# A fused attention and feed-forward kernel: the first half of a weight product as plain float32 matmuls, and the order of the work searched again

## The chip, the cores and the metric

The kernel runs on one core of one Trainium2 chip. The metric is the device time of one execution in microseconds (us), from the runtime, and the median of several runs. A profile of one execution gives the span from the first to the last instruction and every instruction in it. Engines are named as in the profile: PE (matmul; PEld its weight loads), DVE, ACT, POOL, and SP, which here only issues DMAs.

## The reference, cut to what matters

```python
# q, k, v: (4, 8, 576, 64);  S = 576 tokens, D = 64, 4 x 576 = 2304 rows in all
q, k = rotate(q), rotate(k)                          # rotary embedding
attn = softmax(q @ k.T / 8)                          # per batch and head
x = heads_joined(attn @ v)                           # (2304, 512)
x = ((x @ w1) * (x @ w2)) @ w3 @ w_out               # w1, w2 (512, 1024), w3 (1024, 1024), w_out (1024, 512)
out = maximum(maximum(x @ v1, x @ v2), x @ v3) @ v_out   # (512, 768) x 3, then (768, 512)
```

All inputs are used at full precision: the weights reach the kernel as 64-bit words and the result is float32.

## The kernel before

**Products.** Every operand of a large matmul is split into two float32r tiles: HI, a rounded copy (ACT), and LO, what is left over (DVE or POOL, a subtraction). A product is then three matmuls, HI x HI, LO x HI and HI x LO (TERMS, line 42), summed in PSUM. Lines 372 and 373 issue all of them, so that the profile shows them as L373 and the tile names tell them apart. Transposes (L598) are matmuls of float32 tiles against the identity.

**Weights.** convert (line 418) loads a 128 x 512 chunk of 64-bit words into the tile raw (L376, 512 KB; two buffers), turns it to float32 in the tile cw by one ACT and two DVE instructions (L435, L437, L439), makes HI by an ACT copy (L441) and LO by a POOL subtraction (L443; later weights use DVE). Each raw buffer can be loaded again only when the DVE instruction L439 has read it.

**The fold.** Since nothing lies between w3 and w_out, the kernel multiplies these two first. The first half (fold, line 463) covers 512 of the 1024 inner columns: eight row blocks, each of four steps of three 128 x 512 matmuls, 96 in all, into the PSUM tile m. It reads four chunks of w_out (tiles wob in slots 4 and 5, named ws in the rows) and eight of w3 (w3b in slots 0 to 3). Its result goes to memory (wp_d) and the second half (fold_rest, line 764) adds to it much later. The same slots then take w1 and w2.

**Attention.** 16 pairs of heads are worked off one after the other. prepare (line 517) loads q and k and rotates them (tiles qk, and early for pair 1) into st; score (line 567) makes 128 x 576 scores in the tile s (two buffers of two PSUM banks each), of which DVE takes the maximum (L590, into sm) and ACT the exponential (L593, into p); move (line 620) transposes p into PSUM and splits it into pt (ACT L636, DVE L637); values (line 641) multiplies by v (L561 makes v's low part) into pv. inverse (line 600) turns the sums in sm into reciprocals (L603, L605) and transposes them. The first halves of the feed-forward layer (gates, line 486) run between the attention pieces, and the second layer follows after 480 us.

**The order.** Every instruction is a task with an engine, a modelled duration and a number prio. Plan.order (line 193) plays the tasks against the modelled engines and always takes the ready task with the smallest prio; the order in which tasks are taken is the order on each engine and in SP's queue, and every engine works strictly in that order. Plan.issue (line 281) first changes the prio numbers by a list of recorded random moves (MOVES, line 46; move, line 84), which an earlier search had found.

Of the kernel before, what the change touches and what calls it, by code (L numbers as in the profile page):

```python
# [10 lines left out]
F32 = mybir.dt.float32  # L11
F32R = mybir.dt.float32r
U32 = mybir.dt.uint32
AF = mybir.ActivationFunctionType
ALU = mybir.AluOpType
# [26 lines left out]
TERMS = ((HI, HI), (LO, HI), (HI, LO))  # L42
# [1 line left out]


MOVES = (
# [24 lines left out]
)  # L71


def draws(seed):
    mask = (1 << 64) - 1
    s = (seed * 0xD1342543DE82EF95 + 1) & mask
    while True:
        s = (s + 0x9E3779B97F4A7C15) & mask
        z = ((s ^ (s >> 30)) * 0xBF58476D1CE4E5B9) & mask
        z = ((z ^ (z >> 27)) * 0x94D049BB133111EB) & mask  # L80
        yield z ^ (z >> 31)


def move(prio, place, seed):

    d = draws(seed)

    def uni():
        return (next(d) >> 11) * (1.0 / 9007199254740992.0)

    by = (0.1, 0.3, 0.6, 1.5)[next(d) >> 62]
    share = (0.01, 0.03, 0.1, 0.3)[next(d) >> 62]
    parts = (1, 8, 32, 128)[next(d) >> 62]
    width = len(prio) / parts
    lo = uni() * (len(prio) + width) - width
    hi = lo + width
    if parts == 1:
        share *= 0.3
    for i in range(len(prio)):
        if lo <= place[i] < hi and uni() < share:  # L100
            x = uni() + uni() + uni() + uni() - 2.0
            prio[i] = prio[i] + by * 1.7 * x
# [33 lines left out]
class Plan:  # L136
# [6 lines left out]
    LAT = {"PE": 0.05, "ACT": 0.035, "DVE": 0.035, "POOL": 0.08, "SP": 0.1, "HOST": 0.0}  # L143
# [49 lines left out]
    def order(self, prio):  # L193

        tasks, LAT, LAP = self.tasks, self.LAT, self.LAP
        left = [len(k.deps) + len(k.after) for k in tasks]
        ready = [0.0] * len(tasks)
        users, last, slot = {}, {}, {}
        free, wait, live = {}, {}, {}
        for k in tasks:  # L200
            for b in k.shared:
# [2 lines left out]
                live[b.ring] = 0  # L204
                free.setdefault(b.ring.share, [(0.0, n) for n in range(b.ring.share.slots)])
                wait.setdefault(b.ring.share, [])
        clock = dict.fromkeys(LAT, 0.0)
        soon = {e: [] for e in clock}
        now = {e: [] for e in clock}
        dma, port, done = 0.0, 0.0, []  # L210
# [3 lines left out]
        while len(done) < len(tasks):  # L214
# [13 lines left out]
            while soon[e] and soon[e][0][0] <= at:  # L228
                n = heapq.heappop(soon[e])[1]
                heapq.heappush(now[e], (prio[n], n))  # L230
            k = tasks[heapq.heappop(now[e])[1]]
# [15 lines left out]
            end = at + k.dur  # L247
# [3 lines left out]
            if e == "PE":  # L251
                end += self.DRAIN
            if k.tail:
                dma = max(dma, end + 0.65) + 1.2 * k.tail
                end = dma + 0.8
            done.append(k)
            for b in k.shared:
# [10 lines left out]
            for o in k.out:  # L268
                t = clock[e] if e == o.eng == "PE" else end + LAT[o.eng]
# [39 lines left out]

def c_mm(n):  # L310
    return max(0.109, 0.013 + 0.000417 * n)


def c_act(n):
# [16 lines left out]
def fused_kernel(ctx, tc, qk, vv, cs, w3t, wo, w12, m2, wo2, out):  # L331
    nc = tc.nc
    pe, act, dve, pool, sync = nc.tensor, nc.scalar, nc.vector, nc.gpsimd, nc.sync
    plan = Plan()
    add = plan.add
# [12 lines left out]
    wpool = sb_pool(ctx, "wpool", side="right")  # L348
# [23 lines left out]
    def mm(o, a, b, start, stop, **kw):  # L372
        pe.matmul(o, a, b, start=start, stop=stop, **kw)  # L373
# [41 lines left out]
    def either(first):  # L415
        return ("DVE", c_dve, dve) if first else ("POOL", c_pool, pool)

    def convert(src, dst, c, prio, ring=None):

        raw, w = (ring or raw_r).new(), cw_r.new()  # L420

        def hi_word():
            return raw.t[:, :, 1]

        def low_word():
            return raw.t[:, :, 0]

        def u():
            return w.t.bitcast(U32)

        def cols():
            return dst.t[:, :, 512 * c:512 * c + 512]

        load(lambda: raw.t, lambda: src.rearrange("p (n t) -> p n t", t=2), 1.46, w=[raw], prio=prio)
        add("ACT", 0.68, lambda: act.activation(w.t, hi_word().bitcast(F32), **SHRINK),  # L435
            r=[raw], w=[w], prio=prio)
        add("DVE", 0.42, lambda: dve.tensor_scalar(low_word(), low_word(), 29, None, ALU.logical_shift_right),  # L437
            part=[raw], deps=raw.writers, prio=prio, lock=True)
        add("DVE", 0.69, lambda: dve.scalar_tensor_tensor(  # L439
            u(), u(), 3, low_word(), ALU.logical_shift_left, ALU.bitwise_or), r=[raw], w=[w], prio=prio, lock=True)  # L440
        add("ACT", c_act(512), lambda: act.copy(cols()[:, HI], w.t), r=[w], part=[dst], prio=prio)  # L441
        eng, cost, on = either(len(cw_r.all) > 28)
        add(eng, cost(512), lambda: on.tensor_tensor(cols()[:, LO], w.t, f32(cols()[:, HI]), ALU.subtract),  # L443
            r=[w, dst], part=[dst], prio=prio, lock=True)

# [8 lines left out]

    wob = [slots[4 + i].new() for i in range(2)]
    w3b = [slots[i].new() for i in range(4)]
    wp_done = []

    FILL = 1000.0
# [1 line left out]
    def fold(f):  # L463
        acc = m_r.new()
        for j in range(4):
            def go(j=j):
                w, o = w3b[f // 2].t, wob[j // 2].t
                for i, (s, t) in enumerate(TERMS):
                    mm(acc.t, w[:, s, 512 * (f % 2) + 128 * j:512 * (f % 2) + 128 * j + 128],
                       o[:, t, 512 * (j % 2):512 * (j % 2) + 512], j == 0 and i == 0, j == 3 and i == 2)  # L470
            add("PE", 3 * c_mm(512), go, r=[w3b[f // 2], wob[j // 2]], w=[acc], prio=6.0 + 2.6 * f)
        r = ga.new()
        add("ACT", c_evac(512), lambda: act.copy(r.t, acc.t), r=[acc], w=[r], prio=-1)
        wp_done.append(load(lambda: wp_d[f], lambda: r.t, 0.73, r=[r], prio=5))
# [241 lines left out]
            attend(p, part)  # L716
    attention = list(plan.tasks)

    for i in range(2):
        for c in range(2):  # L720
            convert(wo[:, 2 * i + c], wob[i], c, 3.0)
    for f in range(8):
        convert(w3t[f][:, 0], w3b[f // 2], f % 2, 17.0 + 2.2 * f)
        fold(f)
    for f in range(8):
        w12_convert(f)
# [390 lines left out]
```

## Time and profile before

| | us |
|---|---|
| three runs | 934.38, 935.26, 936.12 |
| median | 935.26 |
| the profiled execution, its own time | 933.76 |
| its span, first to last instruction | 931.7 |
| PE busy in the span | 892.7 (96%) |
| DVE, ACT, POOL busy | 601.5, 495.5, 397.6 |

The time of an execution is 2.1 us longer than its span. Matmuls are pipelined, so PE's busy time holds their latency where they overlap others, and the pitch from one matmul to the next has to be read from a run of equal matmuls. In the rows below, an entry in brackets is the idle time of an engine just before the row and what ended it.

### The profile page before, as it was taken

To read this page: it belongs to the slowest core of one execution; us is meant where nothing else is said; L and a number is where in the kernel's file an instruction comes from. 1 tells how busy PE (TensorE), PEld (TensorE's weight loads), DVE (VectorE), ACT (ScalarE), POOL (GpSimd) and SP (SyncE) were. 2 spreads that over 40 slices of the span, in tenths; PEclk is the share of its full clock that TensorE was granted. 3 is DMA by queue.
4 is the path that set the end of the run, shared out by engine and by line. 5 is a ranking of instruction groups with operands and counts; after the bars stand their busy time and mean duration, and the time that the engine had idled before them with its cause. 6 is when DMAs were issued, how large, how long until landed. Compare 5 with 4: busy or idle time off the path is not lost.

```text
span 931.7 us, 16391 instructions
## 1 busy us (share of the span) xinstructions
PE 892.7 (96%) x6018; PEld 836.9 (90%) x6018; DVE 601.5 (65%) x1048; ACT 495.5 (53%) x1108; POOL 397.6 (43%) x387
## 2 busy tenths in 40 slices
PE   2788989999999999999999999999999999999998
PEld 1577879998999999999998999999999999999886
DVE  6788888886666676567657233656788478578300
ACT  3688888886666667576655132534423333334411
POOL 2778887787745567352110000434653333232000
PEclk9799999999999999999999999999999999999999
DMA  7244556463322223311048343333333214155511
GB/s 276 85 126 164 177 187 200 128 188 101 100 91 75 69 84 99 100 41 32 27 146 273 117 142 92 103 101 96 91 91 130 63 46 147 46 184 175 214 62 68
DMA packets 61088, 110.32 MB, mean 118 GB/s; under 512 B 6736, under 2 KB 39760, under 8 KB 61008
## 3 DMA queue, kind: packets, MB, share of 16 engines
q1 hardware_dynamic: 61008, 109.28, 36.4%
q8 instruction: 47, 0.77, 0.4%
q14 instruction: 33, 0.27, 0.1%
HBM read 83.76 MB, written 25.50 MB: 117 GB/s over the span
## 4 chain that ended last, share of the span: by engine, by line
PE 86%; DVE 6%; ACT 2%; DMA 2%; issue 2%; POOL 1%; SPq 0%; DVEq 0%; ACTq 0%
PE q L373 46%; PE m L373 17%; PE t L598 9%; PE s L373 7%; PE pv L373 7%; DVE sm L590 1%; DVE pt L637 1%; ACT pt L636 1%; DVE cw L439 1%; DMA qk__118<-in_qk_dram 1%; DMA raw<-in_w_dram 1%; DVE raw L437 1%; DMA wq_d<-fl 1%; DVE early L542 0%; DMA wp<-wq_d 0%
## 5 line engine op out<-in xcount | busy, mean ns | idle before, releaser
L637 DVE TENSOR_TENSOR pt<-t,pt 128x320 fp32r<-128x320 f32 (+3 forms) x256 | 131.9, 527 | 58.4 <-ACT pt L636 54.1
L636 ACT CAST pt<-t 128x320 fp32r<-128x320 f32 (+3 forms) x256 | 112.5, 459 | 52.1 <-PE t L598 36.1
L373 PE MATMUL pv<-pt,v 128*128 128x256 f32 (+1 forms) x576 | 115.4, 317 | 4.5 <-DVE pt L637 3.6
L590 DVE TENSOR_REDUCE sm<-s 128x1 f32<-128x576 f32 x144 | 104.2, 749 | 17.3 <-PE s L373 16.4
L373 PE MATMUL q<-gt,wp 128*128 128x384 f32 x576 | 100.0, 334 | 0.0
L373 PEld LDWEIGHTS q<-gt,wp 128*128 128x128 f32 x576 | 99.8, 188 | 0.0
L373 PE MATMUL s<-st 64*128 64x288 f32 x768 | 74.2, 320 | 21.2 <-ACT st L548 13.1
L373 PEld LDWEIGHTS pv<-pt,v 128*128 128x128 f32 x576 | 83.5, 190 | 11.4 <-DVE pt L637 7.5
L373 PEld LDWEIGHTS s<-st 64*128 64x128 f32 x768 | 56.9, 193 | 35.3 <-ACT st L548 13.1
L959 ACT COPY tmp<-q 128x384 f32<-128x384 f32 x54 | 25.9, 480 | 92.6 <-PE q L373 92.1
L373 PE MATMUL q<-yc__7828,u 128*128 128x384 f32 x378 | 72.2, 340 | 0.0
L373 PE MATMUL q<-yc__8073,u 128*128 128x384 f32 x378 | 71.2, 340 | 0.0
L373 PE MATMUL q<-yc__7521,u 128*128 128x384 f32 x378 | 70.5, 340 | 0.0
L972 POOL TENSOR_TENSOR tmp<-tmp 128x384 f32<-128x384 f32 x27 | 30.2, 1119 | 86.9 <-ACT tmp L959 86.9
L373 PEld LDWEIGHTS q<-yc__8073,u 128*128 128x128 f32 x378 | 67.1, 188 | 0.1
L373 PEld LDWEIGHTS q<-yc__7828,u 128*128 128x128 f32 x378 | 67.2, 188 | 0.0
L373 PEld LDWEIGHTS q<-yc__7521,u 128*128 128x128 f32 x378 | 67.1, 188 | 0.0
L373 PE MATMUL q<-tail,tail 128*128 128x512 f32 x216 | 49.1, 389 | 0.0
L373 PEld LDWEIGHTS q<-tail,tail 128*128 128x128 f32 x216 | 40.5, 188 | 8.4
L985 DVE TENSOR_TENSOR tmp<-q,tmp 128x384 f32<-128x384 f32 x54 | 29.8, 554 | 16.3 <-PE q L373 16.2
L900 POOL TENSOR_TENSOR yx<-yc__7521 128x384 f32<-128x384 f32 x2 | 2.7, 1336 | 88.1 <-DVE yc__7521 L884 85.8
L1045 ACT COPY ga<-q 128x512 f32<-128x512 f32 x18 | 10.6, 588 | 54.8 <-PE q L373 46.7
(1282 smaller groups left out, 2149.9 us busy)
## 6 DMA issues: line engine op xcount, KB each, us to landing
gt<-g_d SPq DMA_DIRECT2D x24, 384.0 KB
raw<-in_m_dram SPq DMA_DIRECT2D x72, 128.0 KB
raw<-in_w_dram SPq DMA_DIRECT2D x16, 512.0 KB
h_d<-top SPq DMA_DIRECT2D x36, 192.0 KB
tail<-h_d SPq DMA_DIRECT2D x36, 192.0 KB
raw<-in_wo_dram SPq DMA_DIRECT2D x12, 512.0 KB
raw<-in_w3t_dram SPq DMA_DIRECT2D x12, 512.0 KB
vr<-in_vv_dram SPq DMA_DIRECT2D x16, 320.0 KB
```

What stands on the lines that cost most here:

```text
L373: pe.matmul(o, a, b, start=start, stop=stop, **kw)
L437: add("DVE", 0.42, lambda: dve.tensor_scalar(low_word(), low_word(), 29, None, ALU.logical_shift_right), part=[raw], deps=raw.writers, pri ...
L439: add("DVE", 0.69, lambda: dve.scalar_tensor_tensor(u(), u(), 3, low_word(), ALU.logical_shift_left, ALU.bitwise_or), r=[raw], w=[w], prio ...
L590: add("DVE", c_dve(S), lambda s=s, col=col: dve.tensor_reduce(sm.t[:, 0, col:col + 1], s.t[:, :, :288], axis=AX.XY, op=ALU.max, negate=Tru ...
L598: pe.transpose(o, x, ident.t)
L636: h = add("ACT", c_evac(n), lambda: act.copy(hi(), t.t[:rows, a:a + n]), r=[t], w=[pt], prio=prio)
L637: add("DVE", c_dve(n), lambda: dve.tensor_tensor(low(), t.t[:rows, a:a + n], f32(hi()), ALU.subtract), r=[t], part=[pt], deps=[h], prio=prio)
L900: k11 = add("POOL", c_pool(TN), lambda z=z, kk=kk: pool.tensor_tensor(z.t[:, 0], f32(yc.t[:, A11, kk, HI]), f32(yc.t[:, A11, kk, LO]), ALU ...
L959: add("ACT", c_evac(TN), lambda: act.copy(d.t, ps(o)), r=[accs[o]], w=[d], prio=prio)
L972: add("POOL", c_pool(TN), lambda: pool.tensor_tensor(s5.t, s1.t, s5.t, ALU.add), r=[s1], w=[s5], prio=prio)
L985: add("DVE", c_dve(TN), lambda: dve.tensor_tensor(e.t, ps(o), e.t, ALU.add), r=[accs[o]], w=[e], prio=prio)
L1045: add("ACT", c_evac(512), lambda acc=acc, o=o: act.copy(o.t, acc.t), r=[acc], w=[o], prio=P2 - 2)
```

## The change

The first half of the fold is computed by plain float32 matmuls: one instruction of 128 x 512 for each step in place of three, 32 in place of 96. convert gets an argument whole, with which the float32 word is written straight into the weight tile; the cw tile, the HI copy on ACT and the LO subtraction on POOL fall away for the twelve chunks of the fold. w_out's half now needs one slot (4) and w3's half two (0 and 1). The prio of w3's chunks goes from 17 + 2.2 f to 3 + 2.2 f, and the planner prices a fold step by a new function, c_whole. The planner's clocks start at 0.7, its DMA price per load changes, move knows a second kind of move (a shift of up to 128 consecutive tasks), and MOVES is a new list. The choice between DVE and POOL for later LO parts falls on the same chunks as before (28 and 16 count different tiles).

```diff
 MOVES = (
-    100000004, 100000005, 100000020, ...
+    30000018, 30000026, 30000042, ...
 )
...
 def move(prio, place, seed):
+    if next(d) >> 63:
+        by, width = (0.3, 1.0, 3.0, 10.0)[next(d) >> 62], 1 << (next(d) >> 61)
+        lo = int(uni() * (len(prio) + width)) - width
+        x = uni() + uni() + uni() + uni() - 2.0
+        for i in range(max(lo, 0), min(lo + width, len(prio))):
+            prio[i] = prio[i] + by * 1.7 * x
+        return
...
-        clock = dict.fromkeys(LAT, 0.0)
+        clock = dict.fromkeys(LAT, 0.7)
...
-                dma = max(dma, end + 0.65) + 1.2 * k.tail
+                dma = max(dma, end + 0.65)
+                dma += (1.9 if dma < 5.0 else 0.9) * k.tail
...
+def c_whole(n):
+    return 0.05 + 4 * 0.000417 * n
...
-    def convert(src, dst, c, prio, ring=None):
-        raw, w = (ring or raw_r).new(), cw_r.new()
+    def convert(src, dst, c, prio, ring=None, whole=False):
+        raw = (ring or raw_r).new()
+        w = None if whole else cw_r.new()
...
+        def word():
+            return dst.t[:, 512 * c:512 * c + 512] if whole else w.t
...
+        if whole:
+            return
         add("ACT", c_act(512), lambda: act.copy(cols()[:, HI], w.t), r=[w], part=[dst], prio=prio)
-        eng, cost, on = either(len(cw_r.all) > 28)
+        eng, cost, on = either(len(cw_r.all) > 16)
...
-    wob = [slots[4 + i].new() for i in range(2)]
-    w3b = [slots[i].new() for i in range(4)]
+    wob = slots[4].new(lambda slot: wpool.tile([128, 2048], F32, tag="ws4_0", name="wo"))
+    w3b = [slots[i].new(lambda slot, i=i: wlow.tile([128, 2048], F32, tag=f"ws{i}_0", name="w3")) for i in range(2)]
...
-                for i, (s, t) in enumerate(TERMS):
-                    mm(acc.t, w[:, s, 512 * (f % 2) + 128 * j:512 * (f % 2) + 128 * j + 128],
-                       o[:, t, 512 * (j % 2):512 * (j % 2) + 512], j == 0 and i == 0, j == 3 and i == 2)
-            add("PE", 3 * c_mm(512), go, r=[w3b[f // 2], wob[j // 2]], w=[acc], prio=6.0 + 2.6 * f)
+                c = 512 * (f % 4) + 128 * j
+                mm(acc.t, w3b[f // 4].t[:, c:c + 128], wob.t[:, 512 * j:512 * j + 512], j == 0, j == 3)
+            add("PE", c_whole(512), go, r=[w3b[f // 4], wob], w=[acc], prio=6.0 + 2.6 * f)
...
-        convert(w3t[f][:, 0], w3b[f // 2], f % 2, 17.0 + 2.2 * f)
+        convert(w3t[f][:, 0], w3b[f // 4], f % 4, 3.0 + 2.2 * f, whole=True)
```

How the instructions moved is shown at three places. Lines after the change are some 20 to 27 higher: L617 is the maximum (L590 before), L664 the low part of pt (L637), L588 that of v (L561), L464 and L466 the two DVE instructions of a weight word (L437, L439), L630 and L632 the reciprocal (L603, L605).

On DVE, in the last score of pair 0, there stood before:

```order
L590 TENSOR_REDUCE sm_175<-s_278 128x1
L637 TENSOR_TENSOR pt_308<-t_299,pt_308 64x256
L590 TENSOR_REDUCE sm_175<-s_279 128x1
L561 TENSOR_TENSOR v_211<-vr_153,v_211 128x10x64
L659 TENSOR_TENSOR x0__292<-pv_303,x0__292 64x256
L437 TENSOR_SCALAR raw_132<-raw_132 128x512
L590 TENSOR_REDUCE sm_175<-s_326 128x1
L439 SCALAR_TENSOR_TENSOR cw_202<-cw_202,raw_132 128x512
L437 TENSOR_SCALAR raw_179<-raw_179 128x512
L590 TENSOR_REDUCE sm_175<-s_327 128x1
```

Now the same two maxima (here of s_300 and s_301) stand there without them:

```order
L464 TENSOR_SCALAR raw_129<-raw_129 128x512
L664 TENSOR_TENSOR pt_285<-t_263,pt_285 128x512
L466 SCALAR_TENSOR_TENSOR wo_171<-wo_171,raw_129 128x512
L664 TENSOR_TENSOR pt_298<-t_289,pt_298 128x512
L617 TENSOR_REDUCE sm_175<-s_300 128x1
L664 TENSOR_TENSOR pt_326<-t_318,pt_326 64x256
L617 TENSOR_REDUCE sm_175<-s_301 128x1
```

Pair 1's v and the first weight word now come earlier on DVE, ahead of the first pt of pair 0:

```order
L464 TENSOR_SCALAR raw_127<-raw_127 128x512
L617 TENSOR_REDUCE sm_175<-s_209 128x1
L588 TENSOR_TENSOR v_224<-vr_201,v_224 128x10x64
L664 TENSOR_TENSOR pt_234<-t_219,pt_234 128x512
```

So the v and raw instructions that stood ahead of the maxima have moved out of the last score into the stretch before the first pt.

On PE, the first matmuls of the fold stood before behind the last transposes of pair 1's first half:

```order
L598 MATMUL t_648<-ident_111,p0__389 64x128
L598 MATMUL t_648<-ident_111,p1__473 64x128
L373 MATMUL pv_597<-pt_603,v_211 128x256
L373 MATMUL m_663<-ws4__177,ws0__558 128x512 x6
L373 MATMUL pv_677<-pt_618,v_211 128x256 x4
L373 MATMUL pv_677<-pt_654,v_211 128x256 x4
L373 MATMUL pv_677<-pt_657,v_211 128x256
```

Now the first two stand one head earlier:

```order
L625 MATMUL t_574<-ident_107,p0__399 128x128
L625 MATMUL t_574<-ident_107,p1__476 128x128
L393 MATMUL m_583<-wo_171,w3_508 128x512 x2
L393 MATMUL pv_596<-pt_539,v_224 128x256 x4
L393 MATMUL pv_596<-pt_563,v_224 128x256 x4
L393 MATMUL pv_596<-pt_581,v_224 128x256
```

The fold starts ahead of the head's values (pv_596) instead of behind those of the first head (pv_597).

On DVE, at the same place, the words of the fold stand so now (raw_547 and raw_566 reuse the buffers of raw_442 and raw_371, whose last readers are the two L466 here):

```order
L466 SCALAR_TENSOR_TENSOR w3_508<-w3_508,raw_442 128x512
L466 SCALAR_TENSOR_TENSOR wo_171<-wo_171,raw_371 128x512
L664 TENSOR_TENSOR pt_539<-t_531,pt_539 128x512
L664 TENSOR_TENSOR pt_563<-t_541,pt_563 128x512
L617 TENSOR_REDUCE sm_384<-s_549 128x1
L686 TENSOR_TENSOR x1__473<-pv_500,x1__473 64x256
L664 TENSOR_TENSOR pt_581<-t_570,pt_581 64x256
L686 TENSOR_TENSOR x1__473<-pv_500,x1__473 64x64
L617 TENSOR_REDUCE sm_384<-s_550 128x1
L464 TENSOR_SCALAR raw_547<-raw_547 128x512
L464 TENSOR_SCALAR raw_566<-raw_566 128x512
L664 TENSOR_TENSOR pt_617<-t_574,pt_617 128x512
```

Two L464 stand in a row with seven instructions between them and the second L466; before, two L437 (raw_560, raw_651) stood in a row a little later, just ahead of L603.

## Rows read from the trace of the kernel before

**Rows 1.** The page's first section: busy us, share of the span, instructions.

```profile
PE 892.7 (96%) x6018; PEld 836.9 (90%) x6018; DVE 601.5 (65%) x1048; ACT 495.5 (53%) x1108; POOL 397.6 (43%) x387
```

**Rows 2.** Busy us of each engine by stretch; the clock is PE's granted share.

```profile
core 0: us, PE busy (x) PEld busy (x) DVE busy (x) ACT busy (x) POOL busy (x), PEclk, DMA share, GB/s
...
13.14:34.00 20.86, 14.10 (x81) 11.11 (x81) 17.77 (x24) 12.85 (x28) 12.46 (x10) 1.00 0.32 128
34.00:38.00 4.00, 1.05 (x11) 0.82 (x11) 3.91 (x6) 1.48 (x4) 2.73 (x4) 0.78 0.29 82
38.00:50.00 12.00, 9.48 (x45) 7.72 (x46) 7.94 (x16) 7.66 (x19) 9.36 (x8) 0.50 0.67 215
50.00:72.20 22.20, 17.53 (x123) 13.64 (x123) 20.68 (x33) 17.46 (x42) 18.44 (x18) 1.00 0.40 124
72.20:124.00 51.80, 51.20 (x358) 43.16 (x360) 44.30 (x76) 45.40 (x111) 44.68 (x35) 1.00 0.50 162
124.00:150.00 26.00, 23.11 (x186) 20.00 (x184) 22.65 (x41) 22.35 (x56) 22.33 (x19) 1.00 0.51 166
150.00:480.00 330.00, 328.92 (x2710) 310.32 (x2708) 228.31 (x439) 229.67 (x576) 179.28 (x162) 1.00 0.30 93
480.00:519.00 39.00, 38.20 (x223) 34.47 (x224) 26.36 (x48) 17.69 (x30) 0.15 (x1) 1.00 0.80 263
519.00:928.00 409.00, 409.00 (x2292) 395.67 (x2292) 223.90 (x366) 135.66 (x240) 107.42 (x129) 1.00 0.34 108
```

**Rows 3.** Timeline of PE, 13 to 73 us: start, length, what, idle before.

```profile
13.14 0.61 PE L373 MATMUL s<-st 64*128 64x288 f32 x2 [13.14 <-ACT st L548]
...
23.12 1.78 PE L373 MATMUL s<-st,z__105 128*128 128x288 f32 x6 [3.38 <-ACT p__208 L593]
...
38.36 0.60 PE L373 MATMUL s<-st 64*128 64x288 f32 x1 [2.97 <-ACT p__349 L593]
...
64.37 1.64 PE L373 MATMUL m<-ws__177,ws__558 128*128 128x512 f32 x6 [0.28 <-DVE pt L637]
...
72.18 0.27 PE L598 MATMUL t<-ident,sm 128*9 128x128 f32 x1 [2.18 <-DVE sm L605]
```

**Rows 4.** Timeline of DVE, 26 to 70 us.

```profile
26.41 1.33 DVE L637 TENSOR_TENSOR pt<-t,pt 128x512 fp32r<-128x512 f32 x2 [2.30 <-ACT pt L636]
...
33.29 1.56 DVE L561 TENSOR_TENSOR v<-vr,v 128x640 fp32r<-128x640 f32 x1
...
35.35 1.30 DVE L437 TENSOR_SCALAR raw<-raw 128x512 uint32<-128x512 uint32 x1
36.68 0.76 DVE L590 TENSOR_REDUCE sm<-s 128x1 f32<-128x576 f32 x1
...
38.29 0.75 DVE L590 TENSOR_REDUCE sm<-s 128x1 f32<-128x576 f32 x1
...
67.06 2.92 DVE L437 TENSOR_SCALAR raw<-raw 128x512 uint32<-128x512 uint32 x2
```

**Rows 5.** Timeline of PE: two transposes, and the last run of 512-wide matmuls.

```profile
50.22 0.27 PE L598 MATMUL t<-ident,p__266 128*128 128x128 f32 x1
50.33 0.27 PE L598 MATMUL t<-ident,p__317 128*128 128x128 f32 x1
...
915.66 12.40 PE L373 MATMUL q<-tail 128*128 128x512 f32 x54
```

**Rows 6.** One fold tile's weight loads: instructions and form | busy, mean ns.

```profile
L373 PEld LDWEIGHTS m<-ws__177,ws__763 128*128 128x128 f32 x12 | 2.1, 188 | 0.4
```

**Rows 7.** Lines L443 (POOL) and L441 (ACT) alone, 0 to 119 us.

```profile
0.00:119.00 119.00, 0.00 (x0) 15.61 (x12) 0.94 0.50 165
...
0.00:119.00 119.00, 7.61 (x13) 0.94 0.50 165
```

**Rows 8.** A weight load in the chain that ended last, ACT's and PE's waits behind it.

```profile
125.39 5.86 DMA raw<-in_w_dram
...
131.34 0.66 ACT L435 ACTIVATE cw<-raw 128x512 f32<-128x512 f32 x1 [2.30 <-DMA raw<-in_w_dram]
...
132.87 0.42 PE L373 MATMUL pv<-pt,v 128*128 128x320 f32 x1 [1.36 <-DVE pt L637]
```

More of the change, by code (lines that the diff above doesn't have):

```diff
@@ L426, in low_word @@
             return raw.t[:, :, 0]
+        def word():
+            return dst.t[:, 512 * c:512 * c + 512] if whole else w.t
         def u():
-            return w.t.bitcast(U32)
+            return word().bitcast(U32)
+        own = dict(part=[dst]) if whole else dict(w=[w])
         def cols():
@@ L434, in convert @@
         load(lambda: raw.t, lambda: src.rearrange("p (n t) -> p n t", t=2), 1.46, w=[raw], prio=prio)
-        add("ACT", 0.68, lambda: act.activation(w.t, hi_word().bitcast(F32), **SHRINK),
-            r=[raw], w=[w], prio=prio)
+        add("ACT", 0.68, lambda: act.activation(word(), hi_word().bitcast(F32), **SHRINK),
+            r=[raw], prio=prio, **own)
+        first = plan.tasks[-1]
         add("DVE", 0.42, lambda: dve.tensor_scalar(low_word(), low_word(), 29, None, ALU.logical_shift_right),
@@ L439, in convert @@
         add("DVE", 0.69, lambda: dve.scalar_tensor_tensor(
-            u(), u(), 3, low_word(), ALU.logical_shift_left, ALU.bitwise_or), r=[raw], w=[w], prio=prio, lock=True)
+            u(), u(), 3, low_word(), ALU.logical_shift_left, ALU.bitwise_or), r=[raw], deps=[first], prio=prio, lock=True, **own)
+        if whole:
+            return
         add("ACT", c_act(512), lambda: act.copy(cols()[:, HI], w.t), r=[w], part=[dst], prio=prio)
-        eng, cost, on = either(len(cw_r.all) > 28)
+        eng, cost, on = either(len(cw_r.all) > 16)
         add(eng, cost(512), lambda: on.tensor_tensor(cols()[:, LO], w.t, f32(cols()[:, HI]), ALU.subtract),
@@ L466, in go @@
             def go(j=j):
-                w, o = w3b[f // 2].t, wob[j // 2].t
-                for i, (s, t) in enumerate(TERMS):
-                    mm(acc.t, w[:, s, 512 * (f % 2) + 128 * j:512 * (f % 2) + 128 * j + 128],
-                       o[:, t, 512 * (j % 2):512 * (j % 2) + 512], j == 0 and i == 0, j == 3 and i == 2)
-            add("PE", 3 * c_mm(512), go, r=[w3b[f // 2], wob[j // 2]], w=[acc], prio=6.0 + 2.6 * f)
+                c = 512 * (f % 4) + 128 * j
+                mm(acc.t, w3b[f // 4].t[:, c:c + 128], wob.t[:, 512 * j:512 * j + 512], j == 0, j == 3)
+            add("PE", c_whole(512), go, r=[w3b[f // 4], wob], w=[acc], prio=6.0 + 2.6 * f)
         r = ga.new()
@@ L717, in fused_kernel @@
     attention = list(plan.tasks)
-    for i in range(2):
-        for c in range(2):
-            convert(wo[:, 2 * i + c], wob[i], c, 3.0)
+    for c in range(4):
+        convert(wo[:, c], wob, c, 3.0, whole=True)
     for f in range(8):
-        convert(w3t[f][:, 0], w3b[f // 2], f % 2, 17.0 + 2.2 * f)
+        convert(w3t[f][:, 0], w3b[f // 4], f % 4, 3.0 + 2.2 * f, whole=True)
         fold(f)
```

55 rows, old and new, of the table MOVES are left out of this document.

## The prediction

> **What bounds the kernel now.** I read the busy table first. PE is busy for 96% of the span, every other engine for two thirds or less [rows 1]. Then the table by stretches: from 519 to 928 us PE has no idle time at all, from 150 to 480 us it has 330.00 - 328.92 = 1.1, from 480 to 519 us 0.8 [rows 2]. So from 150 us on PE sets the time, and whatever PE is late at 150 us it is late at the end. Ahead of 150 us it is not yet so. Nothing runs on PE before 13.14 us [rows 3]; from there it is idle for 20.86 - 14.10 = 6.8 us up to 34, 2.95 up to 38, 2.5 up to 50, 4.7 up to 72.2, 0.6 up to 124 and 2.9 up to 150, in all 20.4 us [rows 2]. Third, the clock in the same table: after the gap at 34 to 38 us the granted clock is 0.50, the lower level of 1.2 GHz, for the whole stretch from 38 to 50 us, in which PE is busy for 9.48 us; at the full level this work would take half, so the gap costs up to 4.7 us more. These 20.4 + 4.7 us are all that an order can win. Last, PE's and DVE's timelines, for who made PE wait: the maxima and exponentials of the scores (3.38 and 2.97 us), the reciprocal (2.18) [rows 3].
>
> **The change part by part.**
>
> *The matmuls.* A run of 54 matmuls of the fold's shape takes 12.40 us; without one latency of 0.39 at its end (53 pitches) that is 12.01 / 53 = 0.227 us each [rows 5]. The 96 that go cost 96 x 0.227 = 21.8 us of PE. What one plain float32 matmul of that shape costs no row shows. The nearest rows on the cheap side are the float32 transposes, which start 0.11 us apart (50.22, 50.33) for 128 columns [rows 5]: for 512 columns 0.44 us, 32 x 0.44 = 14.1, a gain of 7.7. On the dear side, a product of two numbers that each have two parts has four partial products, of which the old form computed three; at the pitch of a pass 4 x 0.227 = 0.91 us, 32 x 0.91 = 29.1, a loss of 7.3. Dearer still, if each of the four had to load its weights in the open at 0.188 us [rows 6]: 4 x 0.415 = 1.66 us, 53.1, a loss of 31.3. I take 0.91: the fold's own row has the same shape and the same operands, while a transpose multiplies by ones and zeros. The Trainium skill (FP8 and Floating Point Precision, Matmul Precision) says that true FP32 takes four passes through the array, which speaks against this change; by it the matmuls cost +7.3, by the transposes' row -7.7, and no row of the kernel before decides it.
>
> *What the conversion saves.* Twelve LO subtractions on POOL go, 15.6 us, and twelve HI copies on ACT, 12 x 7.61 / 13 = 7.0 us [rows 7]. Neither engine is the bound: in the stretch 72.2 to 124 us PE itself has 0.6 us idle [rows 2]. I count them only where a wait passes through them, below. DVE's two instructions per word stay, and SP's loads are as many as before.
>
> *The gap at 34 to 38 us.* Before, DVE makes v (1.56 us) and shifts a weight word (1.30) right ahead of the maximum at 36.68, and more weight work ahead of the second at 38.29 [rows 4]; PE waits 2.97 us for the exponential behind the first [rows 3]. Now these instructions stand ahead of the first pt, where DVE was idle for 2.30 us [rows 4]. That cover is nearly enough: v and one shift need 2.86. The maxima follow the scores directly. Of 2.95 us idle I take 2 away (bounds 1 to 2.95), since a maximum (0.75) and an exponential still lie between two scores. The clock then need not fall: 3 of 4.7 us (0 to 4.7). If the gap returns elsewhere, both terms are gone.
>
> *The start, 13 to 34 us.* PE's first score waits for the same loads and rotations, so the 13.14 us stay. Two rotations of pair 1 have moved ahead of the first maximum, where they delay it by about one instruction, and one fewer stands ahead of the second. I take 1 us of the 6.8 (-1 to 3).
>
> *38 to 50 us.* The waits there are behind maxima and pt at half clock: 1 of 2.5 (0 to 2).
>
> *50 to 72.2 us.* The first fold matmuls run at 64.37 us [rows 3]: words, then the ACT copy, then POOL. Without the last two they can follow DVE directly, and they stand one head earlier, with one more right ahead of the transposed reciprocal, which waited 2.18 us [rows 3] behind two weight shifts of 2.92 us [rows 4]. Filler of 0.91 us a piece covers most of it: 2.5 of 4.7 (1 to 4).
>
> *72.2 to 150 us.* The waits at 126 to 138 us hang on a weight load that lands 5.86 us after its issue and holds ACT for 2.30, PE then for 1.36 [rows 8]. With POOL and ACT lighter and PE with more to do, 1.5 of 3.5 (0 to 3).
>
> *After 150 us* the set of instructions is the same and PE is full: 0.
>
> *The sum.* Won: 2 + 3 + 1 + 1 + 2.5 + 1.5 = 11.0 us (bounds 1 to 19.7). Lost: 7.3. Net -3.7. The profiled execution took 933.76 us, so it would take 930.1; the median of the runs is 1.5 higher, so 935.26 - 3.7 = 931.6 us.
>
> **The rivals.**
>
> *Loads in the way (slower).* Now two weight shifts stand in a row on DVE behind seven instructions, and their loads can only be issued when the two L466 ahead of these have read the buffers. Two pt of 0.67, two maxima of 0.75 and three short ones are some 4.1 us; a load took 5.86 us to land [rows 8]. DVE would then stand for some 2 us, with pt and the next maxima behind it, hence PE. The eight words of w3 go through the two buffers in four such turns: 4 x 2.2 = 8.8, so 931.6 + 8.8 = 940.4. It decides as soon as a load takes longer than DVE's work between. For it: the old kernel shows just this on ACT [rows 8]. Against: POOL and ACT no longer hold a word back, and PE has its filler ready by then.
>
> *Half the gain.* The waits of the first 70 us are replaced by others and only some 7 of the 11 us come: 7.3 is lost, 935 us, no change. For it: DVE does the same work up to the first fold matmul as before, and it is busy 20.68 of 22.2 us from 50 to 72 [rows 2].
>
> *The float32 matmul is cheap.* At the transposes' price the change doesn't pay on PE at all: 935.26 - 11.0 - 7.7 = 916.6.
>
> *The float32 matmul is dear*, with its weight loads in the open: 935.26 - 11.0 + 31.3 = 955.6.
>
> *All the waits go*: 935.26 + 7.3 - 19.7 = 922.9.
>
> **How the numbers follow.** A measurement of this kernel can tell about 0.2%, 1.9 us, from no change. Chances: the forecast, 926.5 to 933.4 us, 0.50; all waits gone, below 926.5, 0.05; cheap matmul 0.04; half the gain, within 1.9 us of 935.26, 0.17; loads in the way or as much lost by another wait, 937.1 to 942, 0.20; dear matmul 0.04. Faster 0.59, same 0.17, slower 0.24. The range 925 to 940.5 leaves out the cheap and the dear matmul and the outer edges of their neighbours, under 0.2.
>
> **What would show it.** In the profile after: fold matmuls with a pitch of 0.91 us (0.44 and 1.66 are the others); no fall of the clock between 38 and 50 us and no PE wait of 2.97 us ahead of pair 0's last exponentials; the first fold matmul before 60 us; PE idle between 13 and 150 us near 12 us instead of 20.4; and 150 to 928 us as long as before. I am wrong if DVE waits for raw loads between 50 and 100 us, if a clock of 0.50 shows up at another place, or if PE is no longer full after 150 us.

## The result and the profile after

| | us, median | ratio to before, 95% interval |
|---|---|---|
| before | 934.8 | |
| after | 944.1 | 1.0104 [1.0077, 1.0132] |
| after, measured again beside other kernels | 948.1 | 1.0154 [1.0112, 1.0195] |
| predicted | 931.6 (925 to 940.5) | 0.996 |

The kernel after is slower by 9 us, where 4 us of gain were forecast. The profiled execution took 945.02 us (before 933.76), 11.3 more. Its table by stretches, with the bounds of [rows 2] (columns: bounds, length, then for each engine busy time and count, at the end the granted clock, the DMA share and GB/s):

```profile
13.14:34.00 20.86, 14.77 (x84) 12.02 (x83) 19.30 (x24) 11.22 (x26) 14.68 (x12) 1.00 0.30 109
34.00:38.00 4.00, 2.77 (x22) 2.15 (x20) 3.56 (x6) 3.90 (x9) 3.30 (x3) 0.95 0.66 176
38.00:50.00 12.00, 10.02 (x69) 8.62 (x68) 11.36 (x22) 8.53 (x23) 9.29 (x9) 0.87 0.59 198
50.00:72.20 22.20, 18.98 (x123) 12.87 (x121) 17.72 (x30) 15.58 (x38) 15.57 (x14) 1.00 0.56 183
72.20:124.00 51.80, 47.91 (x285) 32.43 (x284) 42.17 (x75) 39.27 (x95) 30.25 (x26) 1.00 0.48 158
124.00:150.00 26.00, 23.69 (x174) 18.69 (x173) 19.08 (x34) 19.94 (x50) 17.55 (x18) 1.00 0.36 124
150.00:480.00 330.00, 326.62 (x2677) 306.27 (x2676) 229.93 (x436) 229.41 (x577) 177.62 (x161) 1.00 0.29 92
480.00:519.00 39.00, 37.05 (x245) 34.48 (x244) 19.55 (x39) 14.92 (x30) 1.76 (x2) 1.00 0.55 179
519.00:928.00 409.00, 407.27 (x2275) 392.56 (x2274) 234.12 (x380) 138.06 (x246) 106.78 (x129) 1.00 0.36 115
```

Read the difference of length and PE's busy time, row by row, against [rows 2]. Up to 72.2 us PE is idle less than before, as forecast. The mean granted clock from 38 to 50 us is 0.87 where it was 0.50; it still falls to the lower level of 1.2 GHz, but for the first 3 us of this stretch only:

```profile
38.00:41.00 3.00, 2.50 (x14) 2.15 (x13) 2.88 (x7) 1.03 (x4) 1.62 (x3) 0.50 0.95 315
41.00:50.00 9.00, 7.52 (x57) 6.47 (x57) 8.48 (x15) 7.50 (x21) 7.66 (x7) 1.00 0.47 160
```

From 72.2 to 124 us it is idle for 3.9 us (before 0.6), from 150 to 480 for 3.4 (1.1), from 480 to 519 for 1.95 (0.8), from 519 to 928 for 1.7 (none).

The turning point shows when PE's matmuls are counted off in the timelines: the start of the same work, in us. A pair of heads has 54 score matmuls, so the scores of pair 2 (pairs are counted from 0) start with the 109th. The last two columns are kernels of the experiments, both with after's computation: in the order of before, and in an order made with loads priced at 4.8 us.

| start of | before | after | order of before | priced at 4.8 us |
|---|---|---|---|---|
| the fold | 64.4 | 53.8 | 62.8 | 54.0 |
| scores of pair 2 | 67.7 | 62.4 | 66.6 | 64.7 |
| scores of pair 4 | 123.7 | 126.0 | 128.8 | 119.3 |
| the products of x | 480.4 | 487.1 | 486.2 | 475.4 |
| the products of gt, the gated result | 554.2 | 563.9 | 560.9 | 548.5 |
| the products with v1 to v3 | 654.1 | 664.4 | 660.7 | 648.4 |
| the last product | 853.4 | 863.8 | 860.0 | 847.7 |

After is 5.3 us ahead of before at the scores of pair 2, 2.3 behind at those of pair 4, 6.7 at the products of x and 9.7 at those of gt. The loss is made between 62 and 564 us.

PE's timeline after has the gap of [rows 3] closed: the two waits in front of the scores at 36 us are 0.47 and 0.40 us.

```profile
36.24 0.40 PE L393 MATMUL s<-st 64*128 64x288 f32 x1 [0.47 <-ACT p__332 L620]
37.04 1.35 PE L393 MATMUL s<-st 64*128 64x288 f32 x11 [0.40 <-ACT p__332 L620]
...
65.45 1.88 PE L393 MATMUL m<-wo,w 128*128 128x512 f32 x4
...
71.03 0.33 PE L625 MATMUL t<-ident,p__589 128*128 128x128 f32 x1 [1.75 <-DVE pt L664]
...
71.71 1.02 PE L393 MATMUL m<-wo,w 128*128 128x512 f32 x2
...
109.69 0.33 PE L625 MATMUL t<-ident,p__864 128*128 128x128 f32 x1 [1.98 <-DVE pt L664]
```

The row at 65.45 is the fold. Each float32 matmul stands in the trace as two records (PE has 5986 records, 32 fewer than before, for 32 matmuls in place of 96); four records take 1.88 us, so the pitch of one is (1.88 - 0.59) / 3 = 0.43 us (0.59 is the time of a single one) and a matmul costs 0.86 us. All 32 cost 27.5 us, against 21.8 for the 96 [rows 5].

The waits at 71.03 and 109.69 are new, both for pt from DVE. What held DVE is in its own timeline:

```profile
56.44 0.43 DVE L464 TENSOR_SCALAR raw<-raw 128x512 uint32<-128x512 uint32 x1
57.08 0.43 DVE L464 TENSOR_SCALAR raw<-raw 128x512 uint32<-128x512 uint32 x1 [0.22 <-DMA raw<-in_w3t_dram]
...
61.59 1.76 DVE L466 SCALAR_TENSOR_TENSOR w<-w,raw 128x512 uint32<-128x512 uint32 x1
...
66.24 0.49 DVE L664 TENSOR_TENSOR pt<-t,pt 128x320 fp32r<-128x320 f32 x1
69.91 0.67 DVE L464 TENSOR_SCALAR raw<-raw 128x512 uint32<-128x512 uint32 x1 [3.18 <-DMA raw<-in_w3t_dram]
70.50 0.48 DVE L664 TENSOR_TENSOR pt<-t,pt 128x320 fp32r<-128x320 f32 x1
...
93.38 0.69 DVE L466 SCALAR_TENSOR_TENSOR w<-w,raw 128x512 uint32<-128x512 uint32 x1
...
108.22 1.02 DVE L464 TENSOR_SCALAR raw<-raw 128x512 uint32<-128x512 uint32 x1 [3.32 <-DMA raw<-in_w_dram]
...
126.17 0.43 DVE L464 TENSOR_SCALAR raw<-raw 128x512 uint32<-128x512 uint32 x1 [2.97 <-DMA raw<-in_w_dram]
```

At 61.59 DVE reads the last of a raw buffer; SP issues the next load into it at once, at 63.39, and it lands 6.50 us later. DVE has 3.4 us of other work, then stands for 3.18 us at the word's first instruction, and pt, for which PE waits, is queued behind it. The waits at 108.22 and 126.17 are of the same kind, but for words of w1 and w2 (in_w_dram); the last word of the fold was read at 93.38.

Two lists of the trace of after follow. First the chain of waits: some of the transfers among its longest pieces, from 60 to 130 us and from 150 to 560 us (start, duration, what).

```profile
63.39 6.50 DMA raw<-in_w3t_dram
72.42 4.00 DMA raw<-in_w3t_dram
102.25 5.88 DMA raw<-in_w_dram
121.44 4.63 DMA raw<-in_w_dram
...
153.78 6.64 DMA g_d<-ga
303.30 5.35 DMA qk__3968<-in_qk_dram
...
490.30 6.71 DMA raw<-in_w3t_dram
499.14 6.11 DMA rawc<-in_w3t_dram
507.74 3.74 DMA rawc<-in_w3t_dram
514.00 4.15 DMA g_d<-ga
```

Then the tile raw from 55 to 135 us: how long DVE and ACT sat idle until a weight load had landed (us, times), 14.4 us in all, more than half of it for the words of w1 and w2.

```profile
  DMA raw<-in_w_dram: 8.0, 5
  DMA raw<-in_w3t_dram: 6.4, 6
```

The transfers lie on the path that sets the end, and not the weight words alone: results on their way to memory (g_d), q and k (qk), and the second half of the weights (rawc) at 490 to 512 us. A 512 KB load takes 3.74 to 6.71 us there. The order was made by a planner that takes such a load to land 0.42 + 0.65 + 0.9 x 1.46 + 0.8 = 3.2 us after SP takes it up; the planner of before, with 1.2 in place of 0.9, took 3.6. So the diff has three changes in one: the float32 fold, a new order, and a lower price for all but the first transfers, under which that order was made. The Trainium skill (DMA: Bandwidth & Descriptors, Anatomy of one DMA) gives 2.0 us and the bytes over 436 GB/s for a transfer issued by GpSimd, by estimate also 3.2 us for 512 KB; these loads are issued by SP, and the trace has 3.74 to 6.71 us, so here it would be too little.

### The profile page after: what moved, and what is told of

Its sections match the earlier page's. It is cut to its first block, busy times and chain, and to the rows that moved or that the text cites. A ratio compares the mean times of both kernels' runs of the same rounds, so it can differ in the third digit from the quotient of the medians.

```text
span 943.2 us, 16297 instructions
## 1 busy us (share of the span) xinstructions
PE 901.0 (96%) x5986; PEld 829.6 (88%) x5986; DVE 602.8 (64%) x1048; ACT 487.2 (52%) x1096; POOL 377.6 (40%) x375
## 4 chain that ended last, share of the span: by engine, by line
PE 75%; DMA 10%; DVE 6%; ACT 3%; issue 3%; POOL 2%; SPq 1%; ACTq 0%; DVEq 0%; POOLq 0%
PE q L393 41%; PE m L393 14%; PE t L625 7%; PE pv L393 6%; PE s L393 6%; DMA raw<-in_w3t_dram 2%; DMA g_d<-ga 1%; DMA raw<-in_wo_dram 1%; DVE pt L664 1%; ACT pt L663 1%; DMA raw<-in_w_dram 1%; DMA rawc<-in_w3t_dram 1%; DMA rb<-r_d 1%; SPq L396 1%; DVE cw L466 1%
## 5 line engine op out<-in xcount | busy, mean ns | idle before, releaser
L664 DVE TENSOR_TENSOR pt<-t,pt 128x320 fp32r<-128x320 f32 (+3 forms) x256 | 132.3, 527 | 63.3 <-ACT pt L663 60.0
L617 DVE TENSOR_REDUCE sm<-s 128x1 f32<-128x576 f32 x144 | 104.1, 751 | 19.2 <-PE s L393 18.1
L479 DVE TENSOR_TENSOR gt<-gt 128x768 fp32r<-128x768 f32 x24 | 25.5, 1062 | 36.8 <-ACT gt L478 36.8
L478 ACT CAST gt<-gt 128x768 fp32r<-128x768 f32 x24 | 20.1, 836 | 43.8 <-DMA gt<-g_d 36.8
```

Of the source, the lines that this page charges most:

```text
L478: add("ACT", c_act(n), lambda: act.copy(sel()[:, HI], f32(sel()[:, LO])), r=[dst], part=[dst], prio=prio)
L479: add(eng, c_dve(n) if eng == "DVE" else c_pool(n), lambda: e.tensor_tensor(sel()[:, LO], f32(sel()[:, LO]), f32(sel()[:, HI]), ALU.subtract),
L617: add("DVE", c_dve(S), lambda s=s, col=col: dve.tensor_reduce(sm.t[:, 0, col:col + 1], s.t[:, :, :288], axis=AX.XY, op=ALU.max, negate=Tru ...
L664: add("DVE", c_dve(n), lambda: dve.tensor_tensor(low(), t.t[:rows, a:a + n], f32(hi()), ALU.subtract), r=[t], part=[pt], deps=[h], prio=prio)
```

## Experiments: the matmuls and the order apart

In each, "before" ran on the same chip; ratios are to it.

**The order of before with float32 matmuls.**

```diff
-                for i, (s, t) in enumerate(TERMS):
-                    mm(acc.t, w[:, s, 512 * (f % 2) + 128 * j:512 * (f % 2) + 128 * j + 128],
-                       o[:, t, 512 * (j % 2):512 * (j % 2) + 512], j == 0 and i == 0, j == 3 and i == 2)
+                mm(acc.t, f32(w[:, HI, 512 * (f % 2) + 128 * j:512 * (f % 2) + 128 * j + 128]),
+                   f32(o[:, HI, 512 * (j % 2):512 * (j % 2) + 512]), j == 0, j == 3)
```

> The order of the kernel before, kept instruction for instruction; only the three matmuls of each fold step (96 in all) become one plain float32 matmul (32) on the same tiles, read as float32. The copies to HI and the subtractions to LO stay; what they hold beyond HI is left out of the product, so a part of the computation is changed. Theory 1, the price of the float32 matmuls goes to the end in any order: the trace of after has 0.86 us for each, 32 x 0.86 = 27.5 against 21.8 before, so 934.8 + 5.7 = 940.5. Theory 2, the weight loads are what costs (the new order's wait for them): here the loads are where they were, and PE's longer work hides some of the old waits between 64 and 150 us (about 5 us of idle there), so 936 to 938. Theory 3, the new order is itself the worse one: as theory 1, at most 940.5.

Measured 939.2 us, 1.0066 [1.0045, 1.0088], which is 4 to 8 us more: the 5.7 us read from the trace of after lie in it. In the old order the matmuls' price goes to the end.

**The order of before with the whole change in computation.**

```diff
-        add("ACT", c_act(512), lambda: act.copy(cols()[:, HI], w.t), r=[w], part=[dst], prio=prio)
+        add("ACT", c_act(512), (lambda: None) if whole else lambda: act.copy(cols()[:, HI], w.t), r=[w], part=[dst], prio=prio)
...
-            convert(wo[:, 2 * i + c], wob[i], c, 3.0)
+            convert(wo[:, 2 * i + c], wob[i], c, 3.0, whole=True)
```

> The whole change in what is computed (32 float32 matmuls, no HI copies and no LO subtractions for the twelve words of the fold), in the order of the kernel before. Against the run with the HI and LO work kept, it prices the relief of ScalarE (7.0 us) and GpSimd (15.6 us). If that relief is worth nothing, as PE sets the time, 940.5 or the same as that run; if the waits on words between 50 and 150 us go by it, 936. The kernel after measured 944.1: whatever this run takes less than that is what the order searched anew costs. Theory 1 (price alone): 939 to 941, order 3 to 5. Theory 2 (loads in the way): the same, but with no wait of PE behind a weight load between 60 and 130 us. Theory 3 (order worse by itself, anywhere): the same time, with the order's loss after 130 us.

Measured 938.0 us, 1.0053 [1.0033, 1.0073]. That is 1 us below what was expected of theory 1; "before" took 933.1 us on this chip, 1.7 less than the expectation started from. The relief of ACT and POOL is worth about 1 us as long as the order stays, within the intervals nothing. After is at 1.0104 and 1.0154, so the new order costs some 5 to 9 us although its first 70 us are better. The table of starts has the same: against this run after leads by 4.2 us at the scores of pair 2 and by 2.8 at those of pair 4, and is behind by 0.9 at the products of x, by 3.0 at those of gt and by 3.8 at the last. Here neither DVE nor ACT waits for a weight word between 55 and 135 us, and PE is idle for 2.7 us from 150 to 928 us, in after for 7.1.

**The new order with three cheap matmuls.** Here the fold's product is another one: the words' upper halves, added three times.

```diff
-                mm(acc.t, w3b[f // 4].t[:, c:c + 128], wob.t[:, 512 * j:512 * j + 512], j == 0, j == 3)
+                for i in range(3):
+                    mm(acc.t, half(w3b[f // 4])[:, c:c + 128, 1], half(wob)[:, 512 * j:512 * j + 512, 1],
+                       j == 0 and i == 0, j == 3 and i == 2)
```

> The order of the kernel after, instruction for instruction, with each float32 matmul of the fold replaced by three bfloat16 matmuls on the upper halves of the same words: PE's work of the fold goes back to about 96 x 0.227 = 21.8 us from 27.5, everything else stays. The low halves are left out of the product. Theory 1 (price goes to the end): 944.1 - 5.7 = 938.4. Theory 2 (weight loads decide when the fold's steps run): PE is done sooner and waits for the same loads, so most of it comes back as idle time: 941 to 943. Theory 3 (the losses lie after 150 us): 938.4 as theory 1.

The matmuls are as cheap as before: six take 1.53 us in its trace, a pitch of (1.53 - 0.39) / 5 = 0.23 us. The time is 943.2 us all the same, 1.0118 [1.0079, 1.0157]. In the new order 5.7 us of PE work can go and no gain clear of the noise comes of it; beside after's 1.0154 one of some 3 us would be possible. In the trace the 5.7 us come back in two parts. PE is idle for 21.4 us between 13.14 and 150 us instead of 18.7. And the granted clock is low for longer: 0.51 from 37 to 44 us, with 6.05 us of work, and 0.57 from 71 to 75 us, with 3.52, against 0.50 from 38 to 41 us with 2.50 in after; by estimate from these numbers that costs 3 us more. DVE and ACT stand for weight words for 14.5 us as in after. So in the fold's stretch the new order is not bound by PE's work alone.

**The new order with more buffers for the words.** The first 12 to 20 words use three weight slots, as long as these are free, besides the two buffers.

```diff
-    raw_r = plan.ring(lambda slot: gap.tile([128, 3 * TN], U32, tag=f"raw{slot}", name="raw")[:, :1024].rearrange(
-        "p (n t) -> p n t", t=2), 2)
+    raw_r = plan.ring(lambda slot: (
+        (wpool if slot > 3 else wlow).tile([128, 2048], U32, tag=f"ws{slot}_0", name="raw") if slot > 1 else
+        gap.tile([128, 3 * TN], U32, tag=f"raw{slot}", name="raw"))[:, :1024].rearrange("p (n t) -> p n t", t=2), 2)
...
```

> The order of the kernel after on every engine, but the weight words land in five buffers instead of two as long as the other three are free (the first 12 to 20 words), so a load need not wait until the words two ahead of it have been read. All of the computation is there. Theory 2 (VectorE stands for weight loads that could not be issued sooner, between 60 and 130 us): the waits behind the loads (6.5 and 4.0 us of the chain at 63 and 72 us, 5.9 and 4.6 at 102 and 121 us) shrink, and PE's first 150 us get shorter by 2 to 5 us: 939 to 942. Theories 1 and 3 (price, or order): 944, no change, though the waits for words shrink in the trace. SyncE's queue still issues the loads in the same order.

Measured 941.9 us, 1.0091 [1.0060, 1.0121]. The waits for words fall to 8.6 us, and PE is idle for 15.1 us between 13.14 and 150 us instead of 18.7; between 150 and 519 us it is idle for 6.5 instead of 5.3. Of the 3.6 us won there 1.2 show as idle time further on, and some 1.8, by estimate, go to a lower clock (0.51 from 38 to 45 us, with 6.21 us of work). The weight words alone are not the cause: PE's idle time behind 150 us did not go with them. So theory 1 holds in the old order and not in the new one, theory 2 has a part in the loss, and theory 3, the order, has to be explained.

## Experiments: the price of a transfer

The order was searched anew with the diff's own kinds of random moves, with two things varied: the fold, and when the planner takes a 512 KB load to land.

```diff
-                dma += (1.9 if dma < 5.0 else 0.9) * k.tail
-                end = dma + 0.8
+                dma += (1.9 if dma < 5.0 else 1.2) * k.tail
+                end = dma + 2.0
```

This is the price of 4.8 us (0.42 + 0.65 + 1.2 x 1.46 + 2.0); for 3.6 us the last number is 0.8, for 6.0 it is 3.2. All other transfers shift with it; the planner's other edits are in all of these orders. With the old fold, the three terms and their conversion are put back.

> The computation of the kernel after (32 float32 matmuls, twelve words written straight into place), its order searched anew once more, with one thing changed in the planner: a 512 KB load is taken to land 4.8 us after its issue, near the 4.0 to 6.7 us in the trace of after, where the planner of after takes 3.2 us (and that of before 3.6). Theory L (the order of after was made for transfers that land sooner than they do, and loses its lead in waits behind them): the lead of 8 us at 70 us stays for the most part, VectorE stands less for weight words between 60 and 130 us than the 13.8 us of after, and the chain from 150 to 560 us has less of DMA: 931 to 937 us on a chip where before takes 933. Theory P (the price of the float32 matmuls is what is lost): 939 to 943. Theory O (any order found by a search of mine or of the change's kind is worse than the one of before): 940 to 945.

> The fold of the kernel before (96 matmuls in three terms, words split in high and low parts), its order searched anew with the planner of after, prices of transfers included (3.2 us for 512 KB). PE has 5.7 us less work than in after. Theory L: the same waits behind transfers as in after, 936 to 942, slower than before although the computation is the same. Theory P: no more than before, 925 to 933, since the lead of the first 70 us is there and the price is not paid. Theory O: 936 to 942, as theory L; the run with transfers priced dear tells these two apart.

> The fold of the kernel before, its order searched anew with a 512 KB load taken to land 4.8 us after its issue. Only this price (and the order that it gives) differs from the run with the old fold and loads priced cheap. Theory L: some of the lead of the first 70 us without the waits: 926 to 932, below before. Theory P: 925 to 933, the same as the run with loads priced cheap. Theory O: 936 to 942, slower than before, and no better than loads priced cheap.

> The kernel after, unchanged, on the same chip as the three re-searched kernels, so that they can be compared without a second chip between them. All theories: 1.0104 times before, 942 to 944.

> The computation and the planner of after, the order from a second, independent search under the same prices (a 512 KB load lands 3.2 us after issue). Theory L (what costs is the price of a transfer under which the order was made): 939 to 948, like after, slower than before. Theory S (the order of after was an unlucky draw of its search; the re-searched one with loads dear was a lucky one): anything from 926 to 948, and no trend over the four prices.

> The computation of after, the order searched with the transfer price of the kernel before: 3.6 us for a 512 KB load, the others in proportion. Theory L: between the two prices tried, 932 to 940, and below the order made at 3.2 us. Theory S: no trend, 926 to 948.

> The computation of after, a second, independent search with the load at 4.8 us, as in the run that took 926.9. Theory L: 925 to 931, below before. Theory S: 926 to 948, as likely above as below before.

> The computation of after, the order searched with the load at 6.0 us, the dear end of what the trace shows (4.0 to 6.7). Theory L: 925 to 932: no wait behind transfers is left to take away at more than 4.8 us, and the order keeps a little more distance than needed. Theory S: 926 to 948.

All results, by price (DMA's share of the chain is in each page; words: idle time of DVE and ACT until a load landed, 55 to 135 us; the last column is PE's idle time from 150 to 519 us):

| landing | fold | us | ratio to before | DMA in chain | words, us | PE idle, us |
|---|---|---|---|---|---|---|
| 3.2 | float32, the change | 944.1 | 1.0104 [1.0077, 1.0132] | 10% | 14.4 | 5.3 |
| 3.2 | the same, measured again | 948.1 | 1.0154 [1.0112, 1.0195] | 11% | 13.3 | 6.0 |
| 3.2 | float32, second search | 941.3 | 1.0068 [1.0048, 1.0089] | 9% | 10.6 | 4.6 |
| 3.2 | three terms | 941.4 | 1.0090 [1.0055, 1.0125] | 7% | 5.7 | 4.2 |
| 3.6 | three terms (before) | 934.8 | 1 | 2% | 2.7 | 1.9 |
| 3.6 | float32 | 935.7 | 1.0014 [1.0001, 1.0026] | 3% | 5.4 | 1.4 |
| 4.8 | three terms | 933.2 | 0.9992 [0.9974, 1.0010] | 1% | 0.7 | 1.5 |
| 4.8 | float32 | 926.9 | 0.9928 [0.9906, 0.9951] | 2% | 3.0 | 0.9 |
| 4.8 | float32, second search | 930.0 | 0.9955 [0.9937, 0.9973] | 1% | 1.1 | 0.9 |
| 6.0 | float32 | 927.8 | 0.9920 [0.9900, 0.9940] | 1% | 0 | 1.0 |

The time falls from 3.2 to 4.8 us of landing and then stays, close to what the trace shows for these loads. Every order made at 3.2 us is slower than before, with either fold and in three searches; no order made at 4.8 or 6.0 us is. Theory L holds, and theory S (luck of the search) falls: two searches at one price differ by 3 to 8 us, 3.2 and 4.8 us by 8 (three terms) to 21 (float32), and the two sets do not overlap. Theory O falls with them, since orders of this kind beat the one of before. How long each search ran is not on record. The lists kept 71 to 129 moves, that of the change 341, and its order is the slowest, so more moves are not what makes an order faster. The sizes were not all foreseen: the float32 fold at 4.8 us came out 4 us below the range of theory L, the old fold 1 us above it, and after, measured again, 4 us above its own. The old fold at 3.2 us speaks against theory P: 941.4 us without the dear matmuls. The idle time after 150 us divides the table by itself, 4.2 us and more at 3.2, below 2 elsewhere. (The row of before was made by the earlier planner.)

The share of the chain by engines, from the pages of after, of its computation at 4.8 us, and at 6.0 us:

```profile
PE 75%; DMA 10%; DVE 6%; ACT 3%; issue 3%; POOL 2%; SPq 1%; ACTq 0%; DVEq 0%; POOLq 0%
```

```profile
PE 90%; DVE 3%; DMA 2%; ACT 2%; issue 1%; SPq 0%; POOL 0%; ACTq 0%; DVEq 0%
```

```profile
PE 91%; DVE 5%; ACT 2%; DMA 1%; issue 1%; SPq 0%; ACTq 0%; DVEq 0%
```

The first stretches of after and of its computation at 4.8 us, in the same columns as above:

```profile
13.14:150.00 136.86, 118.14 (x745) 86.79 (x744) 113.18 (x187) 98.43 (x237) 90.63 (x78) 0.99 0.46 152
150.00:519.00 369.00, 363.67 (x2920) 340.76 (x2919) 249.48 (x475) 244.34 (x606) 179.39 (x163) 1.00 0.32 101
```

```profile
13.14:150.00 136.86, 124.05 (x801) 93.95 (x802) 113.33 (x198) 105.41 (x251) 96.07 (x83) 0.98 0.52 166
150.00:519.00 369.00, 368.14 (x2940) 346.26 (x2940) 249.69 (x480) 242.32 (x601) 172.85 (x157) 1.00 0.34 109
```

PE is busy 124.05 of the first 136.86 us instead of 118.14, and idle 0.9 us instead of 5.3 in the next 369. These orders beat both kernels: the float32 fold at 4.8 and 6.0 us of landing takes 0.992 to 0.996 of the time of before. The closed gap at 34 to 38 us is not what makes them faster: at 4.8 us PE is busy there for 1.08 of the 4 us, as little as before.

What stays open is the size of the float32 fold's own worth under a good order. At 4.8 us it is 3 to 6 us faster than the old fold, although PE has 5.7 us more to do; but there is only one search with the old fold, and two with the new one differ by 3 us. That ACT and POOL have 7.0 and 15.6 us less to do may explain it; this was not tried under that order.

## Why the prediction was wrong, point by point

*The matmuls.* Taken at 0.91 us each, a loss of 7.3; measured 0.86, a loss of 5.7. The rule of four passes (the Trainium skill, FP8 and Floating Point Precision, Matmul Precision) and the trace agree: 0.86 is 3.8 times 0.227. The transposes' row was no guide, and no weight load was in the open.

*The gains up to 72 us* came, at about the size forecast. PE's idle time fell by 1.7 us in the gap (forecast 2), 0.7 at the start (1), 0.5 from 38 to 50 us (1) and 1.45 from 50 to 72.2 (2.5). For the clock 3 us were forecast: before, 9.48 us of work at 0.50 lost 4.7 us; after, 10.02 us at a mean of 0.87 lost 1.3, so 3.4 came, though the clock did fall for some 3 us. The first fold matmul runs at 53.84 us, before 60 as named. Together 7.8 of the 9.5 us forecast.

*72.2 to 150 us: the first step that failed.* 1.5 us were to be won, since POOL and ACT were lighter. Idle time rose from 3.5 to 6.2 us. This is the mechanism of the rival "loads in the way": a load of 5.9 us against 4.1 us of work; in the trace 6.50 against 3.4. It shared a chance of 0.20 with other waits of that size. At the two L464 that it names, 56.44 and 57.08 us, DVE stands for only 0.22 us. Of its four waits of 2.2 us (its own numbers give 5.86 - 4.1 = 1.8) one came, 3.18 us at 69.91, and the two others of that size, 3.32 and 2.97, are for w1 and w2. The argument against it was that PE has its filler ready by then. It had: the step at 71.71 is the last of the fold's second row block, whose word DVE had finished at 63.35. But in PE's order it stands behind the transposes that wait, so it filled nothing.

*After 150 us: the second and larger step that failed.* It was put at 0, since the set of instructions is the same and PE is full. Idle time rose there from 1.9 to 7.1 us. The set is the same, but its order is not, and I did not ask what that order was made for: the diff's line that lowers a transfer's price stood in view and got no term and no rival. In the order of before the float32 fold costs 4 to 8 us; in an order searched for it it does not: at 3.2 us the old fold is as slow (1.0090 against 1.0068 to 1.0154), at 4.8 us the float32 fold is the faster one. So it is this line that made the kernel slower, and a price nearer the trace makes it faster.

*The sum as measured*: won 7.8, lost 5.7 (matmuls), 2.7 (72.2 to 150) and 5.2 (after 150), net a loss of 5.8 us of the 11.3 between the two profiled executions. The rest shows in no idle row. A part of it sits in busy time. From the products of x to those of gt PE does the same 480 matmuls in both kernels (a stretch's edges can catch a few of the neighbours); before:

```profile
480.40:554.20 73.80, 73.36 (x480) 69.25 (x481) 34.54 (x62) 24.45 (x45) 0.00 (x0) 1.00 0.58 188
```

and after:

```profile
487.10:563.90 76.80, 74.48 (x482) 68.92 (x482) 36.39 (x65) 24.85 (x46) 0.00 (x0) 1.00 0.57 184
```

Of the 3.0 us more, 1.9 are idle and 1.1 are busy time for the same work, so there may be waits too short to empty PE; for the other 4.4 us that is argued, not shown.

*The signs named ahead.* Two of the three signs of being wrong came: DVE waits for a raw load between 50 and 100 us, and PE is no longer full after 150 us. A clock of 0.50 at another place did not. PE's idle time from 13 to 150 us, put near 12 us, is 18.7.

## What to carry to other kernels

An order that is searched on a model can spend every margin that the model leaves: here the orders made at 3.2 us put readers so close behind their transfers that engines which keep their order stood waiting, and work that was ready stood behind them. Price transfers at what the trace shows under load (here 4 to 6.7 us for 512 KB), and rather above it: 6.0 us cost nothing against 4.8, while 3.2 cost 8 to 21 us. When a diff changes the planner's prices as well as the work, treat the price as an edit of its own, and look for its cost all over the kernel, also where the instructions stay the same.

## What the runs showed of the hardware

A plain float32 matmul of 128 x 512 takes 0.86 us, stands in the trace as two records of 0.43 us, and its weight loads (two, 190 ns each) are hidden. A 512 KB load issued by SP took 3.74 us while all transfers together moved 175 GB/s and 6.71 us while they moved 357, measured in the trace of after from issue to landing. I had not expected this spread to matter once PE was busy for 96% of the span.
